# Attention and S4D, two layers of each: group 1's 32 query and key columns as a block of their own, a value quarter less in front 2, kernel factors from three real products, powers in three loads

## The chip, the cores and the metric

The kernel runs on one core of a Trainium2 chip. The metric is the time of one execution of the whole program on the device, in microseconds. Five engines share the work: TensorE (PE, its weight loads PEld), VectorE (DVE), ScalarE (ACT), GpSimd (POOL) and SyncE (SP). SP and POOL also issue the DMA transfers that are spoken of here, each in the order in which the program gives them.

## The reference

Four steps on one sequence of 2048 rows and 640 columns, in float32. A is attention with 32 heads of 20 columns, B a diagonal state space layer (S4D) whose long kernel is convolved with the sequence:

```python
def A(x):
    q, k, v = heads(x @ wqkv)                       # 32 heads of 20, rows 2048
    p = softmax(einsum("bhqd,bhkd->bhqk", q, k) * 20 ** -0.5)
    return merge(einsum("bhqk,bhkd->bhqd", p, v)) @ wo

def B(u):
    dt = exp(log_dt); A_ = -exp(log_A_real) + 1j * A_imag      # (640, 128)
    C = (C_real + 1j * C_imag) * dt[:, None]
    P = exp((A_ * dt[:, None])[:, :, None] * arange(2048))
    K = 2.0 * einsum("dn,dnl->dl", C, P).real                  # (640, 2048)
    return irfft(rfft(u.T, 4096) * rfft(K, 4096), 4096)[:, :2048].T + u * D_skip

x = x + A(layernorm(x)); x = x + B(layernorm(x))
x = x + A(layernorm(x)); x = x + B(layernorm(x))
```

## The kernel before

**Attention.** `attention` is called once for each of the two layers. Its **front** normalises the rows, transposes them and keeps them split in two halves of 16 bits (`xh`, `xl`), so that a product is made of three passes: high by high, high by low, low by high. It then computes the first 128 columns of queries and keys (`block0`, tile pq, L681) and the first value quarters (`values4`, tile pv, L524). A value quarter is 160 columns, eight heads; `NQ` of the four are made in the front, three in layer 1 and two in layer 2, side by side in one matmul.

The **main loop** goes over 8 groups g of four heads, 4 blocks qb of 512 queries and 16 blocks kt of 128 keys. For each kt there are two rounds j of two heads: `scores` (L775, eight matmuls into S), the exponential on ScalarE (S to pt), and after the second round `values` (L792, sixteen matmuls, pt times V into pa). That makes 128 exponentials for a group and 1024 for a layer, and "wave n" below is the n-th of a group or layer. At the end of a query block pa goes to oc on VectorE; the sums of the softmax are stored (dn<-oc), read back in another shape (dr), inverted on VectorE, stored (dn<-dr), spread over the rows (db), and multiplied into oc, which is then stored (ot). All of these transfers are issued by POOL. The queries and keys of a group (qop, kop) are loaded by SP from memory (qs, ks; qm is the shift of the softmax).

**Fillers.** Between scores and values the program places other work on TensorE (`fill`, `slot`), in a fixed order that a planner (`Plan`) makes while the kernel is built: it adds up a time for each engine and takes the next step when that fits before ScalarE runs out of scores. The planner's times are its own; only the order that comes out of it is in the program. Two kinds of steps compete:

- `jobs`: the other query and key columns, in blocks b of 128 (`qk(b)`, L560). A block is eight units (queries and keys, four row blocks tq each) of 15 steps; a unit goes from the two halves m0 and m1 to qc on VectorE, is split in qhi and qlo and stored by SP (`post`). After its four units `norms` (L488) sums the squares into nsum; `longest` reduces them to the largest norms and `shift` writes qm. Value quarters (`vq(q)`, L524) follow the same way, each made of 32 half steps; `both` interleaves them with a block.
- in layer 1 only, the kernel factors of B (`kgen`, driven by `weave`): powers from memory (wd) come to kpw by one transfer for each of 20 channel groups, issued by POOL (`load_powers`); `expand` makes the table ktab and its negative kneg, `left` (tiles ka, kat) and `right` (kb) the factors on VectorE, `contract` (L314) multiplies them on TensorE in 160 steps, and the result goes to ko and by POOL to kd. If `weave` has nothing else, it goes on until VectorE's planned time runs out.

`AHEAD` is a table of (wave, us of jobs) that tells how much of `jobs` should be spent by a wave before a contraction may be taken. `need` forces blocks: at wave 117 of a group (qb 3, kt 10) whatever the next group's queries and keys need is run at once, and then the loads for that group are issued. Columns 80g to 80g + 79 belong to group g, so with blocks of 128 the groups 0 to 7 need the blocks 0, 1, 1, 2, 3, 3, 4, 4.

After the attention of a layer come the output projection and the convolution by way of transforms as matmuls (L1048 to L1158); the change does not touch them.

All instructions issued through a helper have the line L74 in the profile (L77 in the changed kernel, whose constants are three lines longer), so they are told apart by tile.

## Time and profile before

| | us |
|---|---|
| median of 3 runs | 2762.24 (2761.13 to 2763.07) |
| the profiled execution | 2763.52 |
| its span in the trace | 2761.7 |
| TensorE busy | 2542.2 (92%) |
| ScalarE busy | 2347.8 (85%) |
| VectorE busy | 1469.1 (53%) |
| POOL busy | 818.0 (30%) |
| layer 1: first to last exponential | 114.05 to 1133.0 |
| layer 2: first to last exponential | 1553.85 to 2529.8 |

The span runs from the first to the last instruction of the profiled execution; the trace has the start and length of each instruction, what it waited for, and when each transfer was under way. Busy shares are means over stages with different limits: what the attention stages cost is read within them. The two attention stages hold 1995 of the 2762 us. Front 1 lies ahead of 114 us, output projection, S4D of layer 1 and front 2 between 1133 and 1554, the rest behind 2530.

### The profile page before, as it was taken

Reading aid. Unit: us, or ns where it says so; the run is one execution under the profiler, and the core shown is the slowest. Engines: PE = TensorE matmul, PEld = TensorE weight load, DVE = VectorE, ACT = ScalarE, POOL = GpSimd, SP = SyncE. Lnnn points to the kernel's source line nnn. Section 1 sums busy time; section 2 is a strip of 40 time slices with the busy share of each in tenths; the row PEclk is TensorE's granted clock in tenths of the full one; section 3 lists DMA queues with packets and bytes.
Section 4 is the critical chain, followed back from the end, with each engine's and each line's share of the span. In section 5 each row is a group of like instructions: output and inputs, shape, how many; then the busy total and the mean of one; then the engine's idle time right before and its main releaser. Section 6 shows DMA issues by size and latency. Waiting matters only on the chain.

```text
span 2761.7 us, 117574 instructions
## 1 busy us (share of the span) xinstructions
PE 2542.2 (92%) x51968; PEld 1439.2 (52%) x51968; DVE 1469.1 (53%) x3294; ACT 2347.8 (85%) x2779; POOL 818.0 (30%) x1232
## 2 busy tenths in 40 slices
PE   7898999999999998899999998999999888888998
PEld 3453544444444443677896544544444333335988
DVE  7645778988887870466776333332222100002865
ACT  8797989999999999555665698999999999997464
POOL 1112222333223324300572022222222422222376
PEclk9999999999999999999999999999999999999999
DMA  6512232323222222454542112111211211112365
GB/s 223 169 43 68 55 79 52 84 60 77 55 69 54 56 88 97 132 189 174 198 150 87 33 50 64 55 52 52 55 49 39 69 27 40 36 40 75 107 195 159
DMA packets 179128, 238.65 MB, mean 86 GB/s; under 512 B 36144, under 2 KB 124208, under 8 KB 176816
## 3 DMA queue, kind: packets, MB, share of 16 engines
q1 hardware_dynamic: 143168, 184.44, 20.2%
q0 software_dynamic: 35440, 46.58, 7.6%
q8 instruction: 410, 6.72, 1.0%
q14 instruction: 110, 0.90, 0.1%
HBM read 154.87 MB, written 76.03 MB: 84 GB/s over the span
## 4 chain that ended last, share of the span: by engine, by line
ACT 50%; PE 29%; issue 9%; DVE 7%; DMA 5%; POOL 1%; SPq 1%; ACTq 0%; DVEq 0%; POOLq 0%
ACT pt L74 48%; PE pa L792 4%; PE S L775 3%; PE psv L1148 3%; PE po L1054 3%; PE psy L1158 2%; PE psx L1136 2%; PE psx L1113 2%; PE m L560 1%; PE po L1048 1%; PE pv L524 1%; PE m L314 1%; PE pst L1123 1%; DMA kop<-ks 1%; PE pq L681 1%
## 5 line engine op out<-in xcount | busy, mean ns | idle before, releaser
L74 ACT ACTIVATE pt<-S 128x1024 f32<-128x1024 f32 x2048 | 1929.0, 1041 | 65.9 <-PE S L775 49.4
L792 PE MATMUL pa<-pt,V 64*32 64x512 f32 x16384 | 1096.6, 592 | 0.6 <-DVE oc L74 0.6
L775 PE MATMUL S<-qop,kop 61*32 61x512 f16 x16384 | 868.9, 382 | 145.0 <-ACT pt L74 127.4
L775 PEld LDWEIGHTS <-kop 61*32 61x32 f16 x16384 | 370.6, 90 | 811.0 <-issue 700.9
L74 POOL DMA_DIRECT2D dn<-oc x256 | 124.7, 494 | 822.1 <-DVE oc L74 754.2
L792 PEld LDWEIGHTS pa<-pt,V 64*32 64x32 f32 x16384 | 309.4, 106 | 67.6 <-issue 6.8
L74 DVE COPY oc<-pa 128x512 f32<-128x512 f32 x64 | 44.2, 691 | 395.3 <-PE pa L792 395.2
L74 DVE TENSOR_SCALAR qc<-m 128x512 f32<-128x512 f32 x64 | 44.1, 689 | 288.7 <-PE m L560 288.7
L74 POOL DMA_DIRECT2D db<-dn x256 | 128.8, 509 | 138.8 <-DMA dn<-dr 136.2
L74 DVE TENSOR_TENSOR kb<-ktab 128x512 f32<-128x512 f32 x240 | 155.4, 684 | 3.0 <-PE m L314 3.0
L560 PE MATMUL m<-xh,wh 64*32 64x512 f16 x2560 | 139.2, 380 | 2.2 <-DVE qc L74 2.2
L560 PE MATMUL m<-xh,wl 64*32 64x512 f16 x2560 | 138.7, 378 | 1.2 <-issue 1.2
L560 PE MATMUL m<-xl,wh 64*32 64x512 f16 x2560 | 138.6, 378 | 0.0
L74 POOL DMA_DIRECT2D ot<-oc x256 | 130.3, 516 | 11.3 <-DVE oc L74 8.1
L314 PEld LDWEIGHTS m<-kb,ka 128*32 128x32 f32 x5120 | 79.9, 111 | 102.1 <-issue 64.6
L560 PEld LDWEIGHTS <-wh 64*32 64x32 f16 x5120 | 88.2, 94 | 73.6 <-issue 35.2
L1141 POOL TENSOR_TENSOR t<-t,kb 128x512 f32<-128x512 f32 x80 | 102.0, 1275 | 72.2 <-DVE t L74 71.2
L74 ACT COPY xt<-pst 128x1024 f16<-128x1024 f16 x80 | 81.6, 1022 | 47.2 <-PE pst L1123 46.9
L314 PE MATMUL m<-kb,ka 128*32 128x64 f32 x5120 | 105.9, 224 | 12.0 <-DVE qc L74 12.0
L74 POOL DMA_DIRECT2D dn<-dr x64 | 35.6, 556 | 232.5 <-DVE dr L74 228.7
L1142 POOL TENSOR_TENSOR t<-t,t 128x512 f32<-128x512 f32 x78 | 99.2, 1272 | 7.3 <-DVE t L74 1.3
L970 POOL TENSOR_TENSOR ul<-u,uh 128x640 f16<-128x640 f32 x30 | 45.7, 1540 | 179.6 <-ACT uh L74 179.6
(268 smaller groups left out, 3774.3 us busy)
## 6 DMA issues: line engine op xcount, KB each, us to landing
ka<-kha SPq DMA_DIRECT2D x80, 256.0 KB
kb<-khb SPq DMA_DIRECT2D x80, 256.0 KB
db<-dn POOLq DMA_DIRECT2D x256, 64.0 KB, 2.7
kpw<-wd POOLq DMA_DIRECT2D x20, 576.0 KB, 7.6
qop<-qs SPq DMA_DIRECT2D x256, 40.0 KB
kop<-ks SPq DMA_DIRECT2D x128, 80.0 KB
ot<-oc POOLq DMA_DIRECT2D x256, 40.0 KB, 2.5
otl<-ot SPq DMA_DIRECT2D x32, 320.0 KB
```

What stands on the lines that cost most here:

```text
L74: made = f(out, *a, **k)
L314: chain(te.matmul(ps[32 * j:32 * j + 32, c8, :], a[n // 2][:, ch, :], b[n][:, dd, :], start=(n == 0), stop=(n == 3), tile_position=(0, 32 ...
L560: chain(te.matmul(ps[r][32 * t:32 * t + 32, :], a_[rows, ct, 32 * t:32 * t + 32], m[rows, ct, sl], start=(k == 0), stop=(k == 14), tile_po ...
L775: chain(te.matmul(S[32 * t:32 * t + 32, 512 * r:512 * r + 512], kt_[rows, kc + 32 * t:kc + 32 * t + 32], qt[rows, :], start=True, stop=Tru ...
L792: chain(te.matmul(pa[r][32 * j:32 * j + 32, :], V[rows, kt, VP * h:VP * h + 32], pts[j // 2][rows, 512 * (j % 2):512 * (j % 2) + 512], sta ...
L1054: te.matmul(pos[hf], oh[:, ct, :], m[:, ct, 320 * hf:320 * hf + 320], start=False, stop=(ct == NCT - 1 and m is wol))
L1113: te.matmul(ps[:, r, i, :], e1[:, e, s, r, :], m[:, s, bs], start=(n == 0), stop=(n == 2))
L1136: te.matmul(px, f2[:, f, :], xt[:, k, :], start=(n == 0), stop=(n == 2))
L1141: ge.tensor_mul(t2, t2, kb)
L1142: (ge if g0 else ve).tensor_add(t1, t1, t2)
L1148: te.matmul(pv[:, g].rearrange("p r i c -> p (r i c)"), t1[:, g * P:g * P + P], fa, start=True, stop=True)
L1158: te.matmul(py[:, i, :], eb[:, 4 * i4 + i, r, :], v[:, r, 4 * i4 + i].rearrange("p g c -> p (g c)"), start=(r == 0), stop=(r == 1))
```

## The change

**Block 1 of 32 columns.** The blocks are now (first column, columns) 0, 128; 128, 32; 160, 128; 288, 128; 416, 128; 544, 96, and the groups need the blocks 0, 1, 2, 3, 3, 4, 5, 5. Block 0 and block 1 together hold groups 0 and 1. Block 1 takes queries and keys side by side: its 64 columns lie in the four positions of a unit as two kinds by two row blocks, so it has two units of 15 steps instead of eight. `post`, `norms` and the selection matrix follow that shape. The other five blocks keep their eight units each, but a step of the last has six matmuls instead of eight. Weights come by a list `order` through `fetch`, also those of value quarters.

**A value quarter less in front 2.** `NQ` in layer 2 is 1 instead of 2; the second quarter (`vq(1)`) is made among the fillers with block 2, the third alone behind block 3, the fourth with block 5.

**Three real products.** With left factors a and right factors made of hi and lo parts A and B, the real part was a_re (A_re B_re) + a_re (-A_im B_im) - a_im (A_re B_im) - a_im (A_im B_re): four products on VectorE and four matmuls a channel. It is now the negative of (a_im - a_re) k1 + a_im k2 + a_re k3, with k1 = (A_re + A_im) B_re, k2 = A_re (B_im - B_re), k3 = A_im (B_re + B_im): three products and three matmuls, and ko is filled with the factor -1. The table gets a third plane (the sum of real and imaginary part) and a tile kdif (the difference) in place of kneg.

**Powers in three loads.** `load_powers` puts three transfers of a third each into the list `slow`; they are issued one by one 18, 21 and 24 us of planned time after the end of a query block, or by `expand` if they are still there when it begins.

**The table `AHEAD`** has new numbers.

```diff
--- before.py
+++ after.py
@@ -30,7 +30,10 @@
 NA, NB = 32, 64
 LV = [1.0, 2.0, 4.0, 8.0, 16.0, 32.0, 64.0, 128.0, 256.0, 512.0, 1024.0, 1536.0]
 PB = 7
-AHEAD = ((0, 0.0), (96, 22.0), (352, 47.0), (478, 72.0), (724, 125.0))
+AHEAD = ((0, 0.0), (110, 6.0), (236, 34.0), (364, 61.0), (600, 95.0), (740, 134.0))
+BLOCKS = ((0, 128), (128, 32), (160, 128), (288, 128), (416, 128), (544, 96))
+NBLK = len(BLOCKS)
+NEED = (0, 1, 2, 3, 3, 4, 5, 5)
 WS = 256.0
 LG = 2
 BOUND = 30.0
@@ -239,11 +242,13 @@
...
         def load_powers(k):
-            ge.dma_start(kpw[k % 2].rearrange("p r n d -> p (r n) d"),
-                         wd[:, :, :, k * BC:k * BC + BC].rearrange("p r n d -> p (r n) d"))
-
-        def expand(k, w, tab, neg):
-
+            for r in range(3):
+                slow.append((k, lambda r=r: ge.dma_start(kpw[k % 2][:, r], wd[:, r, :, k * BC:k * BC + BC])))
+
+        def expand(k, w, tab, dif):
...
+                slow.pop(0)[1]()
             bs = slice(k * BC, k * BC + BC)
             lo = [tab[:, r, :, 0:24].rearrange("p d (g k) -> p d g k", k=8) for r in range(2)]
             hi = [tab[:, r, :, 24:28] for r in range(2)]
@@ -256,50 +261,46 @@
...
-            ve.tensor_scalar_mul(neg, tab[:, 1, :, 8:16], -1.0)
-
-        def views(tab, dd, hi, lo, shp):
-            return ([tab[:, r, dd, hi].unsqueeze(3).to_broadcast(shp) for r in range(2)],
-                    [tab[:, r, dd, lo].unsqueeze(2).to_broadcast(shp) for r in range(2)])
-
-        def left(tab, half, out):
+            ve.tensor_add(tab[:, 2], tab[:, 0], tab[:, 1])
+            yield
+            ve.tensor_sub(dif, lo[1][:, :, 0:3:2], lo[0][:, :, 0:3:2])
+
+        def views(tab, dif, dd, hi, lo, shp):
+
+            fa = [tab[:, r, dd, hi].unsqueeze(3).to_broadcast(shp) for r in range(3)]
+            fb = [tab[:, r, dd, lo].unsqueeze(2).to_broadcast(shp) for r in (0, 2)]
+            return (fa[2], fb[0]), (fa[0], dif[:, dd, lo.start // 16].unsqueeze(2).to_broadcast(shp)), (fa[1], fb[1])
+
+        def left(tab, dif, half, out):
 
...
-            fa, fb = views(tab, slice(half * AC, half * AC + AC), slice(24, 28), slice(16, 24), shp)
-            re, im = (p2.tile(shp, F32, name=f"ka{j}") for j in range(2))
+            f = views(tab, dif, slice(half * AC, half * AC + AC), slice(24, 28), slice(16, 24), shp)
+            both_, im, re = (p2.tile(shp, F32, name=f"ka{j}") for j in range(3))
...
+            out.extend(a.rearrange("p d h l -> p d (h l)") for a in (both_, im, re))
+            for o, ab in zip((t, im, re), f):
+                ve.tensor_mul(o, *ab)
+                yield
+            ve.tensor_add(both_, im, re)
             yield
-            ve.tensor_mul(t, fa[1], fb[1])
+            ve.tensor_add(im, im, t)
             yield
-            ve.tensor_sub(re, re, t)
+            ve.tensor_sub(re, t, re)
             yield
...
+        def right(tab, dif, sub, out):
...
-            fa, fb = views(tab, slice(sub * DC, sub * DC + DC), slice(8, 16), slice(0, 8), shp)
-            ts = [p2.tile(shp, F32, name=f"kb{j}") for j in range(4)]
+            f = views(tab, dif, slice(sub * DC, sub * DC + DC), slice(8, 16), slice(0, 8), shp)
+            ts = [p2.tile(shp, F32, name=f"kb{j}") for j in range(3)]
...
-            ve.tensor_mul(ts[0], fa[0], fb[0])
-            yield
-            ve.tensor_mul(ts[1], neg[:, sub * DC:sub * DC + DC].unsqueeze(3).to_broadcast(shp), fb[1])
-            yield
...
+            for o, ab in zip(ts, f):
+                ve.tensor_mul(o, *ab)
...
 
@@ -308,12 +309,12 @@
...
                 plan.on_pe(0.43)
-                for n in range(4):
+                for n in range(3):
                     for j in range(4):
                         ch, dd = DC * (sub % 2) + 4 * c8 + j, 4 * c8 + j
-                        chain(te.matmul(ps[32 * j:32 * j + 32, c8, :], a[n // 2][:, ch, :], b[n][:, dd, :],
-                                        start=(n == 0), stop=(n == 3), tile_position=(0, 32 * j)))
-            evac = lambda: ve.tensor_copy(ko[:, 2 * sub:2 * sub + 2, :], ps)
+                        chain(te.matmul(ps[32 * j:32 * j + 32, c8, :], a[n][:, ch, :], b[n][:, dd, :],
+                                        start=(n == 0), stop=(n == 2), tile_position=(0, 32 * j)))
+            evac = lambda: ve.tensor_scalar_mul(ko[:, 2 * sub:2 * sub + 2, :], ps, -1.0)
             emptied(*((None, evac) if r else (evac,)))
             if sub == BC // DC - 1:
...
@@ -327,6 +328,8 @@
...
             load_powers(k)
+        while slow:
...
...
@@ -459,18 +468,21 @@
...
-                    sy.dma_start(dst[n, b * P:(b + 1) * P, sl], t)
+                    for k in range(m // rows):
+                        u, v = (k // 2, 2 * tq + k % 2) if b == 1 else (w_, tq)
+                        sy.dma_start((ks if u else qs)[n, c0:c0 + rows, 512 * v:512 * v + 512],
+                                     t[rows * k:rows * k + rows])
...
@@ -485,8 +497,16 @@
         def norms(w_, b, ps):
 
             for tq in range(4):
...
+                if b == 1:
+                    r = 32 * (2 * w_ + tq % 2)
+                    rows, sq = slice(r, r + 32), sqs[0][tq // 2]
+                else:
+                    r = 0
+                    rows, sq = slice(0, BLOCKS[b][1]), sqs[w_].pop(0)
+                chain(te.matmul(ps[32 * tq:32 * tq + 32, :], sel[rows, b * H:b * H + H], sq[rows],
+                                start=True, stop=True, tile_position=(r, 32 * tq)))
...
@@ -538,47 +558,64 @@
...
             def qk(b):
-                for w_ in range(2):
+                n, units = BLOCKS[b][1], 2 if b == 1 else 4
+                for w_ in range(1 if b == 1 else 2):
...
+                        fetch()
...
-                                for t in range(4):
+                                for t in range(4 if b == 1 else n // 32):
+                                    u, v = (t // 2, 2 * tq + t % 2) if b == 1 else (t, tq)
                                     for r in range(2):
                                         rows = slice(64 * r, 64 * r + 64)
-                                        chain(te.matmul(ps[r][32 * t:32 * t + 32, :], a_[rows, ct, 32 * t:32 * t + 32],
-                                                        m[rows, ct, sl], start=(k == 0), stop=(k == 14),
+                                        chain(te.matmul(ps[r][32 * t:32 * t + 32, :], a_[rows, ct, 32 * u:32 * u + 32],
+                                                        m[rows, ct, 512 * v:512 * v + 512],
+                                                        start=(k == 0), stop=(k == 14),
                                                         tile_position=(64 * r, 32 * t)))
...
+                    if b != 1:
+                        yield from total(b, w_)
+                if b == 1:
+                    for w_ in range(2):
+                        yield from total(b, w_)
+                fins[b] = longest()
+                later.append((plan.dve + 3.0, lambda: finish(b)))
+                later.sort(key=lambda e: e[0])
+
...
@@ -600,10 +637,22 @@
...
+            wv_, coming_ = [], [1, 0]
+            order = [(b, w_) for b in range(2, NBLK) for w_ in range(2)]
+            order.insert(6, ("v", 3))
+            if not first_layer:
+                order.insert(4, ("v", 2))
+                order.insert(1, ("v", 1))
             yield from qk(1)
-            yield from qk(2)
-            yield from qk(3) if first_layer else both(qk(3), vq(2), 2)
-            yield from both(qk(4), vq(3), 2)
+            if first_layer:
+                yield from qk(2)
+                yield from qk(3)
+            else:
+                yield from both(qk(2), vq(1), 1)
+                yield from qk(3)
+                yield from vq(2)
+            yield from qk(4)
+            yield from both(qk(5), vq(3), 2)
...
@@ -666,8 +715,8 @@
...
-            NQ = 3 if first_layer else 2
...
+            NQ = 3 if first_layer else 1
...
@@ -736,7 +785,7 @@
...
-                    nxt.append(stage(P, P, "w"))
+                    nxt.append(stage((P, D + P), 64, "w"))
...
@@ -836,6 +885,7 @@
...
                 later.extend((plan.dve + n, f) for n, f in (
                     (0.2, sums), (5.0, load), (10.0, invert), (11.0, back), (15.5, spread)))
+                later.extend((plan.dve + n, lambda: slow and slow.pop(0)[1]()) for n in (18.0, 21.0, 24.0))
...
@@ -876,9 +926,9 @@
...
         tail = None
-        every = {4, ("v", 3)}
+        every = {NBLK - 1, ("v", 3)}
         for g in range(H // 4):
...
@@ -903,7 +953,7 @@
...
                     if qb == 3 and kt == 10 and g + 1 < H // 4:
-                        need((0, 1, 1, 2, 3, 3, 4, 4)[g + 1])
+                        need(NEED[g + 1])
...
```

How the order moves, at three places. First VectorE at the first sub-block of the first channel group (ka, kat: left factors; kb: right factors; a later sub-block has the kb rows alone). Before:

```order
L74 SCALAR_TENSOR_TENSOR ka_1563<-ka_1563,kat 128x512
L74 TENSOR_TENSOR kb_1733<-ktab 128x512
L74 TENSOR_TENSOR kb_1734<-kneg,ktab 128x512
L74 TENSOR_TENSOR kb_1735<-ktab 128x512
L74 TENSOR_TENSOR kb_1736<-ktab 128x512
```

and now:

```order
L77 TENSOR_TENSOR ka_1594<-ka_1595,ka_1596 128x512
L77 TENSOR_TENSOR ka_1595<-ka_1595,kat 128x512
L77 TENSOR_TENSOR ka_1596<-kat,ka_1596 128x512
L77 TENSOR_TENSOR kb_1822<-ktab 128x512
L77 TENSOR_TENSOR kb_1823<-ktab,kdif 128x512
L77 TENSOR_TENSOR kb_1824<-ktab 128x512
```

Three right factors are made where four were; the left ones are three tiles instead of two, of six operations as before.

Second, VectorE where block 1 of layer 1 ends: nsum takes the last squares, the two reductions (k) make the largest norms, and mr is the shift. Before, with the third copy of oc (the end of the third query block) 16 rows ahead of the first reduction:

```order
L74 SCALAR_TENSOR_TENSOR qc<-m_4050,qc 128x512
L74 TENSOR_TENSOR sq<-qc 128x512
L74 CAST qhi<-qc 128x512
L74 TENSOR_TENSOR qlo<-qc,qhi 128x512
L74 TENSOR_TENSOR nsum_127<-nsum_127,m_4329 128x512
L74 TENSOR_REDUCE k_4335<-nsum_126 128x1
L74 TENSOR_REDUCE k_4335<-nsum_127 128x1
L74 TENSOR_SCALAR k2m<-k2m 128x2
L74 TENSOR_SCALAR mr<-nsum_126,k2m 128x512
```

and now, where the copy of oc is the first of the layer:

```order
L77 COPY oc<-pa_1254 128x512
L77 TENSOR_TENSOR oc<-oc,pa_1255 128x512
L77 TENSOR_SCALAR ko<-m_2148 128x128
L77 TENSOR_TENSOR nsum_126<-nsum_126,m_2209 128x512
L77 TENSOR_TENSOR ka_2129<-ka_2130,ka_2131 128x512
L77 TENSOR_TENSOR ka_2130<-ka_2130,kat 128x512
L77 TENSOR_TENSOR ka_2131<-kat,ka_2131 128x512
L77 TENSOR_TENSOR nsum_127<-nsum_127,m_2294 128x512
L77 TENSOR_REDUCE k_2300<-nsum_126 128x1
L77 TENSOR_REDUCE k_2300<-nsum_127 128x1
```

The reductions of block 1 have moved two query blocks ahead. The reductions that end the blocks in layer 1 stood behind the copies 3, 8, 13 and 23 of oc (blocks 1 to 4) and stand now behind 1, 5, 10, 15 and 23 (blocks 1 to 5).

Third, POOL around the third query block's end of layer 1 (kpw: powers; dn, dr, db, ot: the softmax sums and outputs; kd: the kernel's store). Before, at the next end of a query block at which a load of powers stands:

```order
L74 DMA kd<-ko 128x8x64
L74 DMA dn<-oc 16x1x32 x4
L74 DMA ot<-oc 20x512 x4
L74 DMA kpw_166<-wd 128x36x32
L74 DMA dr<-dn 128x16
L74 DMA dn<-dr 128x16
L74 DMA db<-dn 32x512 x4
```

and now:

```order
L77 DMA db<-dn 32x512 x4
L77 DMA kpw_166<-wd 128x12x32 x3
L77 DMA dn<-oc 16x1x32 x4
L77 DMA ot<-oc 20x512 x4
L77 DMA dr<-dn 128x16
L77 DMA kd<-ko 128x8x64
L77 DMA dn<-dr 128x16
```

The load of powers stood between the storing of the sums and the reading of dr; its three parts stand behind db, and a store of the kernel stands between dr and the next store.

More of the change, by code (lines that the diff above doesn't have):

```diff
@@ L349, in kgen @@
                     a = []
[L350 removed]
+                    yield from left(tab, dif, sub // 2, a)
                 b = []
[L352 removed]
+                yield from right(tab, dif, sub, b)
                 pend.append((plan.dve, contract, (bs, sub, ko, a, b)))
@@ L487, in norms @@
             for tq in range(4):
-                chain(te.matmul(ps[32 * tq:32 * tq + 32, :], sel[:, b * H:b * H + H], sqs[w_].pop(0),
-                                start=True, stop=True, tile_position=(0, 32 * tq)))
+                if b == 1:
[6 more added lines that the diff above has]
+                                start=True, stop=True, tile_position=(r, 32 * tq)))
+            if b == 1 and w_:
+                sqs[0].clear()
             if b:
@@ L573, in qk, with fetch @@
                     emptied(*((None, evac) if w_ else (evac,)))
-                fins[b] = longest()
-                later.append((plan.dve + 3.0, lambda: finish(b)))
-                later.sort(key=lambda e: e[0])
+            def fetch():
+                if nxt:
+                    ws_.append(nxt.pop()())
+                    if coming_[0] == "v":
+                        wv_.append(ws_.pop())
+                if order and (order[0][0] == "v" or not ws_):
+                    coming_[:] = order.pop(0)
+                    k, n = coming_
+                    nxt.append(stage(2 * D + n * QW, QW, "v") if k == "v" else
+                               stage(n * D + BLOCKS[k][0], BLOCKS[k][1], "w"))
             def vq(q):
-                make = stage(2 * D + q * QW, QW, "v")
-                yield plan.pe + 5.0, 0.0, False, ()
-                w = make()
+                w = wv_.pop()
                 t0 = plan.dve
@@ L1369, in _constants @@
     sg[:, 0], sg[:, 1] = -1.0, 1.0
-    sel = np.zeros((P, NCT, H))
-    for b in range(NCT):
-        for c in range(P):
-            sel[c, b, (b * P + c) // DH] = 1.0
+    sel = np.zeros((P, NBLK, H))
+    for b, (c0, n) in enumerate(BLOCKS):
+        for c in range(P if b == 1 else n):
+            sel[c, b, (c0 + c % n) // DH] = 1.0
     lv = np.array(LV)[None, :]
```

75 lines of the change are left out of this document (33 added, 42 removed).

## The prediction

> **What bounds the kernel now.** I read first how long each group of four heads takes on ScalarE, then one pass of TensorE work within it, then the waits. Asked by stretches for the exponentials alone (columns: stretch, its length, ScalarE busy and count, granted clock, DMA share, GB/s):
>
> ```profile
> 114.05:1133.00 1018.95, 972.46 (x1024) 0.99 0.26 67
> 890.80:1013.85 123.05, 121.22 (x129) 1.00 0.22 53
> 1553.85:2529.80 975.95, 956.20 (x1024) 0.99 0.16 47
> 2174.15:2292.35 118.20, 117.94 (x129) 1.00 0.14 42
> ```
>
> A group is 128 exponentials. The last row is a group of layer 2 in which nothing is filled in: ScalarE is busy throughout, so 118.20 us is the floor of a group and 118.20 / 64 = 1.847 us that of a pair of them (one kt). Eight groups at the floor are 945.6 us. Layer 1 takes 73 us more, layer 2 takes 30 more. Only what lies above the floor can be won there, and layer 1 holds most of it.
>
> One pair of layer 1 with a contraction step, TensorE in order of time (start, length, work, count):
>
> ```profile
> 598.68 0.41 PE L775 MATMUL S<-qop,kop 61*32 61x512 f16 x8
> 598.91 1.04 PE L792 MATMUL pa<-pt,V 64*32 64x512 f32 x16
> 599.77 0.40 PE L775 MATMUL S<-qop,kop 61*32 61x512 f16 x8
> 600.10 0.65 PE L314 MATMUL m<-kb,ka 128*32 128x64 f32 x32
> 600.68 0.41 PE L775 MATMUL S<-qop,kop 61*32 61x512 f16 x8
> ```
>
> Lengths overlap, so starts count. Scores 0.23, values 0.86, scores 0.33, contraction 0.58: 2.00 us, 0.153 above the floor. TensorE sets the pace in every pair that holds a contraction, and there are 5120 / 32 = 160 of them:
>
> ```profile
> L314 PE MATMUL m<-kb,ka 128*32 128x64 f32 x5120 | 105.9, 224 | 12.0 <-DVE qc L74 12.0
> ```
>
> That is 24.5 us of the 73. Group 6 (the 890.80 row), where contractions are the only filler, shows it: 4.85 us over the floor. Next, who waited for whom: ScalarE for the scores, from 225 to 395 us and from 1660 to 1695 us (sum, times, longest).
>
> ```profile
> ACT pt L74 <- PE S L775: 22.3, 9, 6.1
> ACT pt L74 <- PE S L775: 9.9, 6, 5.4
> ```
>
> Where they lie, ScalarE in order of time (the idle time ahead of each run of exponentials in brackets):
>
> ```profile
> 236.03 1.02 ACT L74 ACTIVATE pt<-S 128x1024 f32<-128x1024 f32 x1 [3.50 <-PE S L775]
> 238.16 9.73 ACT L74 ACTIVATE pt<-S 128x1024 f32<-128x1024 f32 x10 [1.11 <-PE S L775]
> 251.06 17.03 ACT L74 ACTIVATE pt<-S 128x1024 f32<-128x1024 f32 x18 [3.18 <-PE S L775]
> 274.24 1.02 ACT L74 ACTIVATE pt<-S 128x1024 f32<-128x1024 f32 x1 [6.15 <-PE S L775]
> ```
>
> ```profile
> 372.02 1.02 ACT L74 ACTIVATE pt<-S 128x1024 f32<-128x1024 f32 x1 [4.86 <-PE S L775]
> ```
>
> The chain of waits, its longest pieces around 243, around 366 and around 1680 us:
>
> ```profile
> 243.15 4.74 DMA kop<-ks
> 248.60 1.94 DMA kop<-ks
> ```
>
> ```profile
> 359.95 1.84 POOL kpw L74
> 361.79 5.57 DMA dr<-dn
> 367.85 1.74 DVE kb L74 x3
> 371.89 1.71 PE pa L792 x16
> ```
>
> ```profile
> 1679.23 4.05 DMA qop<-qm
> ```
>
> These are two kinds. At 236 TensorE stands in `need` for block 1, whose norms wait for VectorE there; the keys of group 1 can only be fetched after that (243), and in layer 2 the same order leads to 1679. At 360 the powers' load is issued ahead of `dr` on POOL, `dr` lands after 5.57 us, VectorE stands in its queue at `dr`, and the factors, the evacuation of qc and TensorE stand behind it; 274 is the same with kd ahead as well. After the stall the values take 1.71 us instead of 0.86: a stall also costs TensorE its pace for a while.
>
> **The change, part by part**, as a sum against the profiled span, 2761.7 us.
>
> *Three products.* A contraction step issues 24 records, not 32: 0.585 x 3/4 = 0.44 us (estimate), the pair 0.23 + 0.86 + 0.33 + 0.44 = 1.86 us. Saved 0.145 x 160 = 23 us. Bounds: 24.5 (no pair can pass the floor) and 0 (a step that does not shorten). I take 23: the step has no visible part that is not the stream of records. A record takes 0.585 / 32 = 18.3 ns now, four of them side by side. The Trainium skill (TensorE: Matmul & The Clock Gate, section Wait — 56ns, not 53.3ns?) says that start to start never drops below about 25 ns however small a matmul is: 24 records would by that need 0.60 us, as long as 32 take here. By that rule the trace should show 0.80 for 32, and it does not.
>
> On VectorE, 80 of 320 products of 0.684 us go, 54.7 us, and the left factors keep six operations:
>
> ```profile
> L74 DVE TENSOR_TENSOR kb<-ktab 128x512 f32<-128x512 f32 x240 | 155.4, 684 | 3.0 <-PE m L314 3.0
> ```
>
> The pieces of VectorE's order in the part on the change show it at the first sub-block. Each of 20 expansions adds that sum of 896 columns (1.2 us by 0.684 for 512) and the difference (0.7), and loses kneg: +38 us at most. VectorE gets 17 us lighter or more. I count none of it, since the pairs above are paced by TensorE; were VectorE the pace, the 17 would be a gain still.
>
> *Block 1 of 32 columns.* q and k share one block of two units; the last block of 96 columns still takes eight. 34 units instead of 32 a layer, that is 2 x 15 steps, and one more pair of norms. A pair with three q steps takes 1.94 us (starts of scores below); less scores and values (0.23 + 0.86 + 0.23) a step is 0.21, so the units are 6.3 us of TensorE. They are spread: a pair with two steps takes 1.73, and the usual mix of both comes to about the floor. So I take 0 in layer 1 and +1 in layer 2; upper bound +7 each.
>
> ```profile
> 2142.56 0.40 PE L775 MATMUL S<-qop,kop 61*32 61x512 f16 x8
> ...
> 2144.50 0.40 PE L775 MATMUL S<-qop,kop 61*32 61x512 f16 x8
> ```
>
> What it buys is the place where group 1's shift is known. By VectorE's order before, the two reductions that end block 1 stand behind the third copy of oc, in the query block just ahead of group 1; now behind the first, two query blocks (some 60 us) earlier. Then nobody stands in `need` for block 1, its columns are stored long before wave 117, and the twenty loads for group 1 go out at once.
>
> What is late next? By the same order block 2 is reduced behind the fifth copy and group 2 begins with the eighth, block 5 behind the 23rd for group 6 at the 24th, as block 4 does before. Only that last one is tight.
>
> *Powers in three loads.* By POOL's order the loads now stand behind db, where POOL has nothing urgent; `dr` is no longer behind one. kd stays in the way at places. Sixty issues instead of twenty cost POOL at most 40 x 1.84 us (the 359.95 row) over more than 900, and POOL has nothing else to do behind db.
>
> Of the 22.3 us that ScalarE waits between 225 and 395, the five rows above are 18.8; I take 18 as gone by these two parts: bounds 11 (the 274 and 372 rows, the powers' alone) and 22. Of layer 2's 9.9, 9; bounds 0, if another load takes its place, and 9.9.
>
> *A value quarter less in front 2.* The longest pieces of the chain of waits there are all TensorE's; below them the load of group 0's shift:
>
> ```profile
> 1528.87 6.47 PE pq L681 x30
> 1535.34 7.76 PE pv L524 x57
> 1544.24 8.30 PE pv L524 x60
> ```
>
> ```profile
> 1549.76 1.42 SPq L74 DMA_DIRECT2D qop<-qm  x5
> ```
>
> 136 ns a matmul of 320 columns; one of 160 columns takes 70 (2134.67 to 2134.74 below). So 60 cost 4.2 instead of 8.2 us. Three of the four sets save 4.0 each; the last one only about 1, because group 0's shift is loaded at 1549.76 and the first scores cannot start much before. Less 2 for evacuations that a shorter set covers less: 11 us; bounds 4 (one set) and 13.
>
> The quarter comes back in layer 2 as 32 half steps in pairs of their own:
>
> ```profile
> 2132.89 0.41 PE L775 MATMUL S<-qop,kop 61*32 61x512 f16 x8
> ...
> 2134.67 0.23 PE L524 MATMUL m<-vl,xh 128*128 128x160 f16 x1
> 2134.74 0.23 PE L524 MATMUL m<-vh,xl 128*128 128x160 f16 x1
> 2134.90 0.41 PE L775 MATMUL S<-qop,kop 61*32 61x512 f16 x8
> ```
>
> 2.01 us a pair; its other half has eight records instead of seven, 0.07 more. That is 0.16 and 0.23 over the floor: 32 x 0.2 = +6. The fill of layer 2 then reaches into group 5, which is the unfilled row of the first fence and has the room. The quarter ends behind the seventh copy of oc, one before group 2 uses it.
>
> **The sum:** -23 (contractions) - 18 (waits of layer 1) - 11 (front 2) - 9 (group 1 of layer 2) + 6 (third quarter) + 1 (units) = -54, a span of 2708. The median of the runs shown, 2762.2, lies 0.5 above the span: **2708 us**.
>
> **Rivals.**
>
> *The step does not shorten* (12 in 100). The contraction is held by something that does not count records, weights for instance. For it: four run side by side, and the scores behind it start 0.33 later, not 0.22. Against it: 18.3 ns a record leave no time in which nothing is issued. Price: the 23 come back, 2731. To this the 25 ns of the Trainium skill would lead as well.
>
> *The waits only move* (16 in 100). Group 2 of either layer, or group 6 of layer 1, waits for its keys as group 1 does now, since ten loads a pair of heads are issued within eleven waves, and kd still holds POOL. For it: block 5's margin; against it: the margins of the other blocks. The 18 and 9 are kept: 2735.
>
> *Slower: the powers come late* (6 in 100). The loads wait in a list until a slot behind db; an expansion that finds them there issues them itself, and VectorE stands until they land, with qc behind it and TensorE behind that. Price per expansion up to the landing time of a load, 7.6 us:
>
> ```profile
> kpw<-wd POOLq DMA_DIRECT2D x20, 576.0 KB, 7.6
> ```
>
> Eighteen expansions at 7.6 are 137 us, 2761.7 - 54 + 137 = 2845; from 3 us each it decides. Against it: by the order the last of each three stands at least one query block (about 30 us) ahead of its expansion. The Trainium skill (DMA: Bandwidth & Descriptors, section Anatomy of one DMA — SWDGE (gpsimd) path) fits one DMA as 2.0 us plus its bytes at 436 GB/s, 3.4 us for the whole load and 2.4 for each third, 7.4 if one follows the other: the split costs latency, and only the cover of 30 us makes it free. No run here shows the thirds.
>
> *Better than forecast* (4 in 100): every bound on its good side, 24.5 + 22 + 13 + 10 - 6 = 63.5: 2698.
>
> **Chances.** Forecast 62, the others as given. The range takes in the corner on the good side with a little room and both rivals that keep part of the loss, all but the slow case: low 2695, high 2742. Runs of this kernel lie within 0.1% of each other, so 0.2% (5.5 us) can be told from no change. Faster: all but the slow case, 94, less 3 for two rivals that meet and for a small loss not seen here. Faster 0.91, the same 0.02, slower 0.07.
>
> **What would show it.** Right: pairs with a contraction at 1.86 us; no stall over 2 us at waves 118, 129, 147 and 243 of layer 1 or 129 of layer 2; layer 1 near 977 us, layer 2 near 974, front 2 some 11 shorter. Wrong: pairs still at 2.0, waits for kop or qop at groups 2 and 6, or VectorE waiting for kpw.

## The result, and the profile after

The median is **2718.7 us** (2717.6 to 2719.2, 4 runs) against 2762.7 before (2761.1 to 2765.1): a ratio of 0.984 (0.982 to 0.986), 44 us less. The forecast was 2708 us, 54 less. By stage, from the two profiled executions (a layer is counted from the start of its first to the start of its last exponential, a microsecond less than in the stretches below):

| stage | before | after | difference | forecast |
|---|---|---|---|---|
| start to first exponential | 114.1 | 115.5 | +1.4 | 0 |
| layer 1, first to last exponential | 1018.0 | 983.2 | -34.8 | -41 |
| from there to front 2 | 343.9 | 339.7 | -4.2 | 0 |
| front 2, first transpose to first exponential | 77.9 | 65.1 | -12.8 | -11 |
| layer 2, first to last exponential | 975.0 | 980.9 | +5.9 | -2 |
| rest | 232.8 | 232.6 | -0.2 | 0 |

Front 2 and the rest did about what was forecast. Layer 1 gave less, layer 2 became slower, and 4.2 us went between the layers, where nothing was forecast. The exponentials by stretches, as in the first view of the prediction (length, ScalarE busy and count, granted clock, DMA share, GB/s):

```profile
115.50:1099.75 984.25, 963.20 (x1024) 1.00 0.26 68
859.50:980.05 120.55, 119.18 (x130) 1.00 0.23 58
1503.45:2485.40 981.95, 959.52 (x1024) 0.99 0.17 47
1751.75:1881.35 129.60, 120.99 (x128) 0.96 0.18 52
2248.55:2366.65 118.10, 118.07 (x129) 1.00 0.15 42
```

The floor of a group has stayed (118.10). Group 6 of layer 1, with contractions alone, lies 2.4 us above it instead of 4.85. The fourth row is new: group 2 of layer 2 takes 129.60, in which ScalarE works 121 us.

TensorE in order of time at two contraction steps of layer 1 (start, length, work, count):

```profile
606.90 0.41 PE L824 MATMUL S<-qop,kop 61*32 61x512 f16 x8
607.24 0.54 PE L315 MATMUL m<-kb,ka 128*32 128x64 f32 x24
607.72 0.41 PE L824 MATMUL S<-qop,kop 61*32 61x512 f16 x8
607.94 1.04 PE L841 MATMUL pa<-pt,V 64*32 64x512 f32 x16
608.80 0.40 PE L824 MATMUL S<-qop,kop 61*32 61x512 f16 x8
```

By starts: contraction 0.48 (0.47 as the median over the layer), scores 0.22, values 0.86, scores 0.33: 1.89 us, not 1.86.

Who waited for whom, ScalarE for the scores (sum, times, longest), in the whole of layer 1, first before and then after:

```profile
ACT pt L74 <- PE S L775: 35.3, 27, 6.1
```

```profile
ACT pt L77 <- PE S L824: 16.6, 21, 1.3
```

And after, from 225 to 395 us and from 1735 to 1765 us:

```profile
ACT pt L77 <- PE S L824: 6.1, 7, 1.3
ACT pt L77 <- PE S L824: 9.7, 4, 5.4
```

No wait in layer 1 is longer than 1.3 us now, and their sum fell from 35.3 to 16.6. In layer 2 the wait of 9.9 us at group 1 has gone and one of 9.7 stands at group 2. There the chain of waits runs over two loads of keys, and SyncE, in order of time, shows what came ahead of them:

```profile
1743.54 5.11 DMA kop<-ks
...
1749.90 5.13 DMA kop<-ks
```

```profile
1691.74 48.64 SPq L77 DMA_DIRECT2D ws<-in_wqkv  x2
1740.43 1.32 SPq L77 DMA_DIRECT2D qs<-qhi  x1
1741.80 0.43 SPq L77 DMA_DIRECT2D qs<-qlo  x1
1742.33 2.31 SPq L77 DMA_DIRECT2D kop<-ks  x4
1744.69 1.09 SPq L77 DMA_DIRECT2D qop<-qs  x2
```

```profile
SPq L77 <- DVE wl L77: 43.7, 1, 43.7
```

SyncE stood for 43.7 us (its longest wait there, for wl on VectorE: the last line) at the load of a value quarter's weights: since the change these share one buffer ws with the weights of query and key columns, which VectorE has to read first. Then came a store of a finished unit, and only then, at 1742.33, the twenty loads of group 2, whose first exponential was due at about 1749 (the first load went 3.8 us behind wave 117, and eleven exponentials take 0.923 us each). From the first to the last of the twenty pass 11.5 us here.

### The profile page after: what moved, and what is told of

It reads as the page before. It is cut to its first block, busy times and chain, and to the rows that moved or that the text cites. A ratio compares the mean times of both kernels' runs of the same rounds, so it can differ in the third digit from the quotient of the medians.

```text
span 2717.1 us, 115609 instructions
## 1 busy us (share of the span) xinstructions
PE 2534.4 (93%) x50944; PEld 1445.2 (53%) x50944; DVE 1477.0 (54%) x3292; ACT 2337.4 (86%) x2762; POOL 852.6 (31%) x1282
## 4 chain that ended last, share of the span: by engine, by line
ACT 49%; PE 30%; issue 9%; DVE 7%; DMA 4%; POOL 1%; SPq 0%; ACTq 0%; DVEq 0%; POOLq 0%
ACT pt L77 47%; PE pa L841 5%; PE S L824 3%; PE psv L1198 3%; PE po L1104 3%; PE psy L1208 2%; PE m L578 2%; PE psx L1186 2%; PE psx L1163 2%; PE po L1098 1%; PE pst L1173 1%; PE pkf L1078 1%; DMA kop<-ks 1%; PE pv L544 1%; PE pq L730 1%
## 5 line engine op out<-in xcount | busy, mean ns | idle before, releaser
L824 PE MATMUL S<-qop,kop 61*32 61x512 f16 x16384 | 880.4, 381 | 125.4 <-ACT pt L77 105.1
L77 DVE TENSOR_SCALAR qc<-m 128x512 f32<-128x512 f32 (+1 forms) x68 | 46.9, 689 | 296.4 <-PE m L578 296.4
L578 PE MATMUL m<-xh,wh 64*32 64x512 f16 x2560 | 146.7, 379 | 1.4 <-DVE qc L77 1.4
L578 PE MATMUL m<-xh,wl 64*32 64x512 f16 x2560 | 147.3, 378 | 0.0
L578 PE MATMUL m<-xl,wh 64*32 64x512 f16 x2560 | 145.5, 377 | 0.0
L544 PEld LDWEIGHTS <-xh 128*128 128x128 f16 x960 | 79.6, 98 | 50.9 <-issue 35.6
L77 DVE TENSOR_TENSOR kb<-ktab 128x512 f32<-128x512 f32 x160 | 106.3, 682 | 0.0
L77 DVE TENSOR_SCALAR V<-m 128x160 f32<-128x160 f32 x64 | 20.7, 324 | 156.3 <-PE m L544 156.3
L77 DVE TENSOR_SCALAR dr<-dr 128x16 f32<-128x16 f32 x64 | 11.0, 171 | 171.8 <-DMA dr<-dn 171.6
```

The source lines that it names most:

```text
L77: made = f(out, *a, **k)
L544: chain(te.matmul(ps[:, :n], a_[:, ct, sl], m[:, ct, :], start=(k == 0), stop=(k == 14)))
L578: chain(te.matmul(ps[r][32 * t:32 * t + 32, :], a_[rows, ct, 32 * u:32 * u + 32], m[rows, ct, 512 * v:512 * v + 512], start=(k == 0), stop ...
L824: chain(te.matmul(S[32 * t:32 * t + 32, 512 * r:512 * r + 512], kt_[rows, kc + 32 * t:kc + 32 * t + 32], qt[rows, :], start=True, stop=Tru ...
```

## The experiments

All medians are of runs beside the kernel before, which lay at 2764 to 2765 in these (2762.7 with the first result): a difference to the 2718.7 of after is sure to about 2 us. The trace of one execution is less sure: layer 1 of two kernels below that differ in layer 2 alone takes 984.4 and 988.7 us. For each start of a group two numbers were read from the traces: when SyncE issues its first load, against wave 117 of the group before (the exponential after which the program asks for them), and what the group loses there (from four exponentials ahead of its first to four behind it, less 8 x 0.923 us, the floor). Before, the seven starts of layer 1 lose 8.5 us together and those of layer 2 9.9; after, 5.1 and 14.1.

**One part undone.** Four products again, on TensorE as below and on VectorE as before:

```diff
-                for n in range(3):
+                for n in range(4):
...
-                        chain(te.matmul(ps[32 * j:32 * j + 32, c8, :], a[n][:, ch, :], b[n][:, dd, :],
+                        chain(te.matmul(ps[32 * j:32 * j + 32, c8, :], a[n // 2][:, ch, :], b[n][:, dd, :],
```

> The changed kernel with the four products of before on VectorE and TensorE; blocks, value quarters, three loads and the table stay changed. A: a step is a fixed 0.136 us plus 14 ns a record (32 records 0.584, 24 records 0.472 in the two traces), so each of 160 steps takes 0.112 us longer: 2718.7 + 18 = 2737, contraction pairs at 2.00 us, few other waits. B (VectorE was the pace, and 17 us more work there brings waits back): ScalarE waits over 5 us longer in layer 1, 2745 or more. C (the step does not set the pace): 2719 to 2722.

2746.9 us, 28 more than after. The step is back at 0.584 us, which is A's 18, but the time is B's (2745 or more), and so are the waits: ScalarE waits 31.9 us for scores in layer 1 instead of 16.6. What came back lies at starts of groups, which lose 18.5 in layer 1 instead of 5.1. At group 3 (VectorE's last reading of the old weights in ws, then SyncE in order of time; ScalarE's waits from 484 to 506 us):

```profile
480.39 0.83 DVE L77 SCALAR_TENSOR_TENSOR wl<-ws,wh 128x640 f16<-128x640 f32 x1
```

```profile
481.25 0.38 SPq L77 DMA_DIRECT2D ws<-in_wqkv  x1
481.68 0.52 SPq L77 DMA_DIRECT2D qs<-qhi  x1
482.25 0.42 SPq L77 DMA_DIRECT2D qs<-qlo  x1
482.77 2.32 SPq L77 DMA_DIRECT2D kop<-ks  x4
```

```profile
ACT pt L77 <- PE S L828: 8.2, 3, 6.6
```

SyncE stood 19.4 us at the load of weights, until VectorE had read the old ones; the store behind it was ready, and the loads came after both. The first load goes 1.8 us ahead of wave 117; in the changed kernel it goes 6.7 us ahead. So VectorE's work does count, but by where the planner puts other steps: that VectorE is the pace of this layer, as B has it, is not shown. A kernel below with the same four products loses 4.7 us at the starts of layer 1 once the loads go ahead of the stores.

The staging buffer:

```diff
-            ts = tag + "s" if pool else "ws"
+            ts = "ws" if first_layer and not pool else tag + "s"
```

> The changed kernel with a staging buffer for weights of query and key columns and one for those of value quarters in layer 2, as before the change; layer 1 keeps the shared one. A: the wait of 9.7 us where group 2 of layer 2 begins comes from SyncE standing 44 us at the load of a value quarter's weights into the shared buffer, with group 2's ten loads behind it: the wait goes, 2709 (2708 to 2712), group 2 of layer 2 at about 121 instead of 129.6 us. B (block 2 itself is late, or issuing twenty loads in eleven waves is too long in any case): group 2 stays near 129, 2717 to 2720.

2719.1: no gain, and group 2 takes 128.7 us, which is B's number. The load no longer blocks SyncE, but the store behind it still does (it waits 44.1 us for qhi on VectorE):

```profile
1739.01 0.34 SPq L77 DMA_DIRECT2D qs<-qhi  x1
1739.73 0.34 SPq L77 DMA_DIRECT2D qs<-qlo  x1
1740.17 2.30 SPq L77 DMA_DIRECT2D kop<-ks  x4
```

The first load went from 3.8 us behind wave 117 to 0.4 ahead, and group 2 loses 6.3 instead of 10.2. Group 5, whose first load is 0.5 ahead in both, lost 2.9 there and 6.2 here: where the load goes as late, the loss still scatters by some microseconds.

Two value quarters in front 2:

```diff
-            NQ = 3 if first_layer else 1
+            NQ = 3 if first_layer else 2
...
-                order.insert(1, ("v", 1))
...
-                yield from both(qk(2), vq(1), 1)
+                yield from qk(2)
```

> The changed kernel with two value quarters in front 2 as before; the second is not filled in any more. A: front 2 (first transpose to first exponential of layer 2) 13 us longer, back at 72 us; layer 2 loses the quarter's 24 pairs over the floor, 6 us; the shared staging buffer still blocks SyncE, but ahead of group 3 instead of group 2, so that between 0 and 9.7 us of that wait go: 2718.7 + 13 - 6 - (0 to 9.7) = 2716 to 2726. B (the quarter costs nothing in layer 2 because the room is there): 2731. C (front 2's gain is of another part): front 2 under 63 us, below 2716.

2730.1: the quarter is worth 11.4 us. That is 4 us above A's range and near B's 2731. Front 2 took 78.1, 13.0 more, as A says. Layer 2 got only 2.1 shorter: its starts lose 19.6 instead of 14.1, now with group 2 behind a store and group 3 behind the shared buffer. Less these 5.5 us it would be 7.6; a comparison without such losses comes below.

One load of powers:

```diff
-            for r in range(3):
-                slow.append((k, lambda r=r: ge.dma_start(kpw[k % 2][:, r], wd[:, r, :, k * BC:k * BC + BC])))
+            ge.dma_start(kpw[k % 2].rearrange("p r n d -> p (r n) d"),
+                         wd[:, :, :, k * BC:k * BC + BC].rearrange("p r n d -> p (r n) d"))
```

> The changed kernel with one load of powers for a channel group, issued where the generator stands, as before. A: the load stands ahead of dr at places again, and VectorE, qc and TensorE wait behind it: two or three waits of 4 to 6 us in layer 1 come back, 2718.7 + 11 = 2730 (2727 to 2735). B (the waits went with the move of block 1 alone): layer 1 within 2 us of 983, 2717 to 2721.

2727.0, 8.3 more: the lower end of A's range, but not at A's place. No wait came back at waves 147 or 243, nor in the kernels below that have the new blocks and one load. Group 0 takes 132.1 instead of 124.5, with one wait at wave 17, because VectorE waits once for the first load of all (before the change it was 9.7 us, after it 5.5 in two waits):

```profile
DVE kpw L77 <- DMA kpw<-wd: 11.2, 1, 11.2
```

Over all traces ScalarE waits 2.7 to 6.4 us at wave 17 with one load, 0.9 to 3.2 with three, and not at all in the one trace of the changed kernel. Of the 8.3 us, 2.3 lie in layer 2, whose program is the same in both, and are scatter.

**One part alone, on the kernel before**, and the third product left out. The three loads, with `load_powers` as in the change:

```diff
                 later.extend((plan.dve + n, f) for n, f in (
                     (0.2, sums), (5.0, load), (10.0, invert), (11.0, back), (15.5, spread)))
+                later.extend((plan.dve + n, lambda: slow and slow.pop(0)[1]()) for n in (18.0, 21.0, 24.0))
```

> The kernel before with the powers in three loads alone. A (the forecast): the two waits at waves 147 (6.3 and 1.1 us) and 243 (5.0 and 1.2) of layer 1 shrink, the others stay: 2762 - 11 = 2751 (2749 to 2755). B (without the change of blocks other work meets dr, and the waits move): 2760 to 2765.

2758.2, a ratio of 0.9973 (0.9962 to 0.9985). It lies between A and B, and both mechanisms are there: the waits at waves 147 and 243 fell from 6.3 and 5.0 to under 1.3, and the starts of layer 1 lose 25.2 instead of 8.5: 8.0 at group 1 (3.8 before), 8.5 at group 2 (1.4) and 5.2 at group 5 (1.0). Groups 2 and 5 stood behind a store before too. Group 2's first load now goes 0.2 us ahead of wave 117 instead of 2.2. Group 5's goes 3.5 ahead, no later than before (3.0); there the three loads of powers go out on POOL among the twenty, and a load of keys takes 8.12 us on the chain of waits:

```profile
749.41 3.10 POOL L74 DMA_DIRECT2D kpw<-wd  x3 [1.00 <-issue]
```

```profile
750.33 8.12 DMA kop<-ks
```

The blocks alone are the changed kernel with products, quarter and loads undone as above.

> The blocks (32 columns apart), the order of weights and the table of the change, with four products, one load of powers and two value quarters as before. A (the forecast): the waits of group 1 in layer 1 (8 us) and layer 2 (9 us) go, one comes for the units: 2762 - 16 = 2746. B (from the three kernels in which one part was undone, which cost 28, 11 and 8 us, 47 in all, more than the whole gain of 44): the blocks alone bring nothing, new waits at groups 2, 3 and 5 take the place of group 1's: 2762 to 2768.

2768.9, a ratio of 1.0010 (0.9998 to 1.0022): B in substance, a microsecond above its range. Group 1 loses 1.1 and 1.5 us in the two layers instead of 3.8 and 8.4, as forecast, but all starts together lose 19.4 and 19.5. Group 3 of layer 2 now stands behind the shared buffer (SyncE from 1924 us, wave 117 at 1921.1; ScalarE's waits from 1918 to 1945 us):

```profile
1924.42 0.40 SPq L77 DMA_DIRECT2D ws<-in_wqkv  x1
1924.91 2.30 SPq L77 DMA_DIRECT2D kop<-ks  x4
```

```profile
ACT pt L77 <- PE S L827: 10.0, 3, 6.0
```

The changed kernel with a step of 16 records (its result lacks a product):

```diff
-                for n in range(3):
+                for n in range(2):
...
-                                        start=(n == 0), stop=(n == 2), tile_position=(0, 32 * j)))
+                                        start=(n == 0), stop=(n == 1), tile_position=(0, 32 * j)))
```

> The changed kernel without the third product on TensorE, whose matmuls are left out (VectorE still makes all factors): 16 records in a step. A: a step is 0.136 us fixed and 14 ns a record, 0.36 us; a pair would take 1.78 us and ScalarE sets the pace at 1.85: 160 x 0.043 = 7 us less, 2712 (2710 to 2714). B (VectorE or the transfers, not TensorE, hold the pairs above the floor): 2717 to 2720.

2710.3: A. TensorE in order of time:

```profile
606.81 0.41 PE L824 MATMUL S<-qop,kop 61*32 61x512 f16 x8
607.16 0.43 PE L315 MATMUL m<-kb,ka 128*32 128x64 f32 x16
607.57 0.41 PE L824 MATMUL S<-qop,kop 61*32 61x512 f16 x8
```

The pair takes 1.83 us, and the next scores wait for ScalarE; where they do not, the step is 0.36 (the shortest tenth of the steps). Layer 1 is 7 us shorter, as A says. With three products TensorE still set the pace.

**The loads ahead of the stores.** The stores that do not belong to the next group are held back for a few kt (`outs` holds the stores to come, `hold` starts as `[False]`), and layer 2 has its own staging buffer as above:

```diff
-            while outs and (end or outs[0][0] <= plan.pe):
+            while outs and (end or not hold[0] and outs[0][0] <= plan.pe):
...
+                    hold[0] = qb == 3 and 4 <= kt <= 10 and g + 1 < H // 4
...
                             load_q(g + 1, j, 0)
+                        hold[0] = False
```

> The changed kernel with its own staging buffer for value quarters in layer 2, and with the stores of a finished unit (qhi, qlo) held back from kt 4 of a group's last query block until the next group's twenty loads are issued. A: what a group loses at its start follows from when SyncE gets to its first load: 6.5 us ahead of wave 117 costs 0.1 to 0.5, 0.5 us ahead costs 3 to 6, 3.8 us behind costs 10; in layer 2 groups 2 and 5 stood behind such a store. Both then start 6.5 us ahead: 10.2 + 2.9 - 0.6 = 12.5 us less, 2706 (2704 to 2709). B (the transfers of the loads themselves are slow there, whatever stands ahead of them on SyncE): groups 2 and 5 lose 5 or more still, 2714 to 2720.

**2706.6 us**, a ratio of 0.979 (0.977 to 0.980): A, 12 us under after and faster than both kernels. In layer 2 (SyncE at group 2; then the exponentials of the layer and of group 2 by stretches):

```profile
1733.39 2.31 SPq L77 DMA_DIRECT2D kop<-ks  x4
1735.75 1.09 SPq L77 DMA_DIRECT2D qop<-qs  x2
...
1746.35 0.35 SPq L77 DMA_DIRECT2D qs<-qhi  x1
1746.80 0.59 SPq L77 DMA_DIRECT2D qs<-qlo  x1
```

```profile
1504.90:2475.10 970.20, 959.18 (x1024) 1.00 0.18 48
1750.20:1873.60 123.40, 120.81 (x129) 1.00 0.19 52
```

The loads go 6.6 us ahead of wave 117, the store waits until they are out, and the starts of layer 2 lose 1.5 us instead of 14.1. Layer 1 did not gain (988.7 us, 984.25 after); group 4 of it loses 4.3 although its loads go 6.7 us ahead. There too the three loads of powers go out, at 603.21, among the twenty, and a load of keys takes 6.49 us on the chain. With the shared buffer kept:

> The changed kernel with the loads ahead of the held stores, and the shared staging buffer kept in layer 2. A: group 5 of layer 2 (behind a store) is free of its 2.9 us, group 2 (behind the load into the shared buffer, which waits for VectorE) loses 5 to 10 still: 2711 to 2716. B (the buffer does not matter once the stores are held): 2706.

2715.5: A. Group 5 loses 0.3, group 2 still 9.1, with its first load 1.9 behind wave 117. So at group 2 both had to go, the store and the buffer. The same hold on the blocks alone, with the buffer split, tests why they had brought nothing:

> The blocks alone (four products, one load, two quarters), with the loads of a group ahead of the held stores and own staging in layer 2. A (the blocks brought nothing because new groups stood behind a store): groups 2, 3, 5 of layer 1 and 2, 3 of layer 2 lose 1.8, 6.1, 8.5, 6.0 and 10.3 us now; with the loads ahead nearly all of it goes: 2769 - 31 = 2738 (2734 to 2748), and the blocks have then their forecast gain. B (the blocks cost something else): 2755 or more.

2737.8: A, 27 us under the kernel before. The starts lose 4.7 and 2.7 in the two layers. Layer 2 of this kernel differs from that of the 2706.6 us in the value quarter alone, and it takes 967.4 us instead of 970.2: the quarter costs 2.8 us there. And on the kernel before:

> The kernel before with the stores held back behind the loads alone. A (group 1 waits for its own block, whose stores cannot be held): the 3.8 and 8.4 us that group 1 loses at its start in the two layers stay, 2760 to 2764. B (there too it is the order on SyncE alone): both go, 2750 to 2753.

2761.4, a ratio of 0.9989 (0.9978 to 1.0): A. Group 1's loss does not go; it is 8.4 and 8.9 where it was 3.8 and 8.4. Its first load follows the last store of its own block, 4.7 and 3.1 us behind wave 117.

One attempt went no further, the planner's cost of a step cut by a quarter, at all three places where it stands:

```diff
-                plan.on_pe(0.43)
+                plan.on_pe(0.33)
...
```

> The version with the loads ahead, in which the planner also counts a contraction step as 0.33 us instead of 0.43, since the step is a quarter shorter. A (TensorE's work is the same and sets the pace): only places move, 2703 to 2710. B (the planner's slack of 0.1 us a step leaves TensorE idle somewhere): 2695 to 2701.

2710.9: no gain, a microsecond above A's bound and far from B. (The step itself had become a fifth shorter, 0.584 to 0.472, not a quarter.)

Over all fourteen traces and their 196 starts of groups:

| first load against wave 117 | starts | lost, mean (range), us |
|---|---|---|
| over 6 us ahead | 155 | 0.5 (0.1 to 4.3) |
| 4 to 6 ahead | 9 | 1.1 (0.1 to 1.8) |
| 2 to 4 ahead | 6 | 2.1 (1.0 to 5.2) |
| 0 to 2 ahead | 13 | 6.0 (2.9 to 9.3) |
| behind | 13 | 8.9 (3.8 to 10.3) |

When the loads go is not all of it. Of the 90 starts in layer 1 whose first load goes over 2 us ahead, 48 have a load of powers issued between 6 us before that first load and 11 us after it; they lose 1.2 us on average and up to 5.2, the other 42 lose 0.5 and up to 2.0. That the powers' transfers slow those of the keys fits this, but no run tests it.

## Why the prediction came out as it did

The time lies in the range that was stated, 11 us above the forecast. The two steps that failed are a cost (the contraction step, 5 us) and a wait (the loads of later groups, 8 us in layer 2). That 4.2 us went between the layers, where no term stood, hid part of it by luck.

*Three products, -23.* The mechanism was right, the size was not. The failing step is "0.585 x 3/4 = 0.44 us": it took a step for a stream of records with no fixed part. Steps of 32, 24 and 16 records take 0.584, 0.472 and 0.36 us, so 0.136 are fixed and a record costs 14.0 ns. Saved were 160 x 0.112 = 18 us. That VectorE's lighter load counts for nothing was wrong in another way: with four products the starts of groups lost 13 us more, because other work on VectorE moves the ends of units.

*Waits of layer 1, -18.* They fell by 18.7 us, and for group 1 by the reason given: "the twenty loads for group 1 go out at once". For the 11 us at waves 147 and 243 the reason is not shown: the three loads alone take them away on the kernel before, but with the new blocks they are gone with one load as well. VectorE's waits for `dr` did not even get shorter (29.5 us before, the longest 5.7; 34.7 after, the longest 12.8); they no longer reach ScalarE.

The step that failed is that the other blocks had room, read from the order of the reductions on VectorE ("Only that last one is tight"). A group can wait although its block is finished: its loads stand in SyncE's queue behind whatever store or weight load was put there before, also of another block, and SyncE waits there for VectorE. So the blocks alone brought nothing and the three loads alone 6 us. In layer 1 all parts together happened to put the ends of units away from wave 117; that was luck, and the kernel with four products does not have it. With the loads ahead of the stores the blocks gave 27 us under the kernel before, 24 of it against the kernel before with the same hold.

*Front 2, -11.* The number was right, 12.8, and undoing the quarter gives 13.0 back. The split was not the one forecast (three sets and a little of the last): the chain of waits shows two sets at half their length, and the last set is off it, because the shift's reductions and loads run beside it:

```profile
1477.69 3.94 PE pv L544 x57
1490.74 3.96 PE pv L544 x57
1495.07 1.29 DVE nsum L77 x2
1501.41 1.19 DMA qop<-qm
```

*Group 1 of layer 2, -9.* It went (8.4 to 0.2) and came back as 10.2 at group 2 and 2.9 at group 5; a wait for keys at group 2 was one of the stated signs of being wrong. This is the rival "The waits only move", which had 16 in 100; it named group 2 but put the cause in ten loads issued within eleven waves and in kd. It was the order on SyncE: with the loads ahead, and the buffers apart, the two lose 0.2 and 0.3.

*The third quarter, +6, and the units, +1.* The quarter cost 7.6 us by the subtraction above, which leaves the starts of groups aside, and 2.8 where the loads go ahead in both kernels. The second compares two traces as they are; by it the term was twice too large. The units were not tested on their own.

*Powers late (the slow case).* It did not come: the thirds land after 4.8 us (median from issue), and VectorE waited 5.5 us in all for powers in layer 1 (9.7 before). The Trainium skill (DMA: Bandwidth & Descriptors, section Anatomy of one DMA — SWDGE (gpsimd) path) fits one DMA as 2.0 us plus its bytes at 436 GB/s, by which an estimate for a third is 2.45 us; the page of this profile shows twice that:

```profile
kpw<-wd POOLq DMA_DIRECT2D x60, 192.0 KB, 4.8
```

*What stays open:* The stretch between the layers takes 338 to 340 us in all profiles with the new blocks and 341 to 345 in the three with the old ones; why was not looked for. What the three loads give in the changed kernel, up to 8 us, was seen at the first load and not at `dr`. And whether the powers' transfers hold up the keys' at the starts of layer 1 was not tested.

## What to carry to other kernels

A queue that issues in order is a wait of its own: before a step is moved, read what stands ahead of the loads it feeds, and what that waits for, not only when the data are ready. If a planner fills gaps, put loads with a deadline ahead of stores without one; otherwise each edit reshuffles which load is late, and parts measured alone neither add up nor mean much. Look also at what else moves data while such loads run. Cost a shorter burst by its fixed part and its slope, from two lengths if the trace has them.

## What the runs showed of the hardware

In a contraction step four matmuls (128 rows by 32, 64 columns) start within 20 ns on the four positions, the next four 80 ns after the first, and every later four 56 ns after the four ahead of them (medians of both kernels), which is 14.0 ns a record. From the start of the last record to the next scores pass 149 ns. So steps of 16, 24 and 32 records take 0.136 us and 14.0 ns for each record.

SyncE takes 0.55 to 0.58 us to issue one load of keys or queries (2.31 for four, 1.09 for two) and 0.25 for one of the shift. From the first to the last of the twenty loads of a group mostly pass 11 to 13 us (11.5 at group 2 above), more than the 10.2 of the eleven exponentials that were meant to cover them.
